# Letting GpSimd take turns between the passes of two score tiles, with eight constants of the planner set anew, in a window attention kernel whose score tiles are shared by three engines

## The chip, the cores and the metric

One core of a Trainium2 chip. The metric is the device time of one execution in microseconds (us), lower is better. The kernel before takes 1082.78 us (median of 3 runs, 1082.43 to 1082.89).

## The reference

Cross-shaped window attention on a 224 x 224 image with 96 channels. Half of the channels attend within horizontal stripes of 8 rows, half within vertical stripes of 8 columns; each stripe has 1792 tokens.

```python
qkv = einsum('bhwc,cd->bhwd', x, wqkv)             # x: (1, 224, 224, 96) bf16
# per direction: 28 stripes of 8*224 = 1792 tokens, 48 channels
a = softmax(einsum('bqc,bkc->bqk', q, k) * 48**-0.5)
o = einsum('bqk,bkc->bqc', a, v)
# ... the two halves are put side by side ...
return einsum('bhwc,cd->bhwd', o, wo)
```

What matters here: the scores' exponential. Two stripes are worked on together, and their scores are cut into tiles of 128 partitions x 1024 values; there are 28 pairs x 49 = 1372 such tiles.

## The kernel before

A planner inside the kernel runs when the program is built. It keeps a modelled time for each engine, picks the next instruction of each, and so writes one fixed order per engine with semaphore waits. A score tile goes to one of three engines:

- ScalarE ("a"): one exponential instruction out of PSUM.
- VectorE ("d"): an approximation in four passes over the tile, which stays in PSUM banks 4 and 5 meanwhile.
- GpSimd ("p"): VectorE copies the tile from banks 4 and 5 into a z buffer in SBUF, and GpSimd makes six passes there.

The last pass writes the bits of a bf16 number as an integer; a second matmul then multiplies the tile with V.

```python
NZP = 2                                            # z buffers
zp_sb = [sb(f"zp_sb{i}", [128, 1024], FP32) for i in range(NZP)]
up_sb = sb("up_sb", [128, 1024], FP16)             # one set of scratch
uq_sb = sb("uq_sb", [128, 1024], FP16)
# ...
def add(eng, waits, fn, occ=100.0, done=None, mode=None):
    # ... occ: how long the plan has the engine taken;
    # without done, the result is visible to others at occ + 100 ns
# ...
def p_dur(k):                                      # planned ns of a GpSimd pass
    return 1047.0 if k in (0, 2, 5) else 2130.0

def p_step(e, k, zi, sl):                          # pass 1 is k == 0
    z = zp_sb[zi][:]
    frac = zp_sb[zi][:].bitcast(U16)[:, 0:2048:2]
    u, q = up_sb[:], uq_sb[:]
    if k == 0: return e.tensor_scalar(u, frac, PS / U, PS * PA, ALU.mult, ALU.add)
    if k == 1: return e.tensor_tensor(q, u, u, ALU.mult)
    if k == 2: return e.tensor_scalar(q, q, 1.0, PB, ALU.mult, ALU.add)
    if k == 3: return e.tensor_tensor(u, q, u, ALU.mult)
    if k == 4: return e.tensor_tensor(z, z, u, ALU.add)
    return e.tensor_scalar(PTP[sl][:].bitcast(U16), z, 1.0, PC, ALU.mult, ALU.add)

def pick_pool():                                   # t is the plan's time
    # ... an output addition first, if one is ready ...
    if pow_q:
        p = pow_q[0]                               # the oldest tile, until it is done
        if vis(p["ev"]) > t:                       # its last pass isn't visible yet
            return False
        # ... plan pass p["k"], waiting for p["ev"] ...
```

GpSimd also makes the output additions ("L647") of the second, vertical half. Numbering of the passes: pass 1 to 6 are L983, L985, L987, L989, L991, L992 in the kernel before. In the changed one they are L985, L987, L989, L991, L993, L994, and the copy is L1037 in place of L1033.

The softmax here doesn't subtract the row's maximum and nothing guards it: scores larger than these inputs give would overflow.

## Time and profile before

| | before |
|---|---|
| time, median | 1082.78 us |
| span of the profiled run | 1081.0 us |
| score tiles: ScalarE / VectorE / GpSimd | 1161 / 117 / 94 |
| ScalarE's exponentials, busy and idle before them | 1064.7 us and 1.9 us |
| GpSimd busy | 959.3 us |

The tile counts are the counts (x...) of the exponential, of VectorE's first pass and of GpSimd's first pass. GpSimd's waits in the kernel before (who waited for whom: total us, times, longest us):

```profile
POOL up_sb L983 <- DVE zp_sb L1033: 47.7, 6, 38.6
POOL out_sb L647 <- DVE tmp L624: 22.3, 26, 4.4
```

38.6 us of the first line is the one wait for the very first tile. What is left, 9.1 us for copies and 22.3 us for output additions, is nearly all that the view puts down to other engines in the rest of the run (TensorE adds 1.3 us).

### The profile page before, as it was taken

The numbers are of one execution on the slowest core, as the hardware profiler recorded it, in microseconds if no ns is written. First come the engines' busy times: TensorE is split into PE (matmuls) and PEld (weight loads), VectorE is DVE, ScalarE is ACT, GpSimd is POOL, SyncE is SP. The second block draws the span as 40 slices with busy tenths as digits, with TensorE's granted clock in tenths as the row PEclk, the third lists the DMA queues.
The fourth block names the chain that finished last, engine by engine and source line by source line (L and its number), as shares of the span: only waits on it lengthen the run. The fifth ranks groups of instructions, "written<-read, shape, count | busy, mean of one in ns | idle before, by whom it ended". The sixth has DMA issues, their size and how long they took to land.

```text
span 1081.0 us, 28395 instructions
## 1 busy us (share of the span) xinstructions
PE 1030.4 (95%) x12065; PEld 374.3 (35%) x12065; DVE 1025.8 (95%) x1411; ACT 1066.9 (99%) x1164; POOL 959.3 (89%) x662
## 2 busy tenths in 40 slices
PE   9999999999999999999999999999999999999997
PEld 3333333333333333333333333333333333333332
DVE  6999999999999999999999999999999999999997
ACT  7999999999999999999999999999999999999997
POOL 0499999989998999998998999999999999999995
PEclk9999999999999999999999999999999999999999
DMA  5301101110110121011011222222222222221111
GB/s 98 76 6 36 36 10 27 36 28 10 36 36 11 26 36 19 18 36 21 19 34 32 39 42 41 40 41 41 40 42 40 39 43 40 39 42 37 34 22 33
DMA packets 168999, 37.35 MB, mean 35 GB/s; under 512 B 168872, under 2 KB 168872, under 8 KB 168872
## 3 DMA queue, kind: packets, MB, share of 16 engines
q1 hardware_dynamic: 167256, 35.35, 17.1%
q8 instruction: 94, 1.54, 0.6%
q10 hardware_dynamic: 1616, 0.18, 0.1%
q14 instruction: 33, 0.27, 0.1%
HBM read 0.15 MB, written 9.63 MB: 9 GB/s over the span
## 4 chain that ended last, share of the span: by engine, by line
ACT 97%; SPq 1%; PE 0%; DMA 0%; DVE 0%; issue 0%
ACT PTA L892 97%; SPq L205 1%; DMA xT_sb<-in_x_dram 0%; PE ps L853 0%; PE ps L198 0%; DVE tmp L624 0%; DVE out_sb L647 0%; PE ps L612 0%; PE ps L1176 0%; DVE OT_sb L943 0%; PE ps L467 0%; DVE rc L618 0%; PE ps L724 0%
## 5 line engine op out<-in xcount | busy, mean ns | idle before, releaser
L892 ACT ACTIVATE PTA<-ps 128x1024 bf16<-128x1024 f32 x1161 | 1064.7, 1290 | 1.9 <-PE ps L198 1.9
L198 PE MATMUL ps<-QT_sb,KT_sb 49*64 49x512 bf16 (+3 forms) x5488 | 476.3, 363 | 43.3 <-ACT PTA L892 32.2
L853 PE MATMUL ps<-PTA,V_sb 128*64 128x512 bf16 (+1 forms) x2648 | 412.1, 365 | 0.2
L194 PEld LDWEIGHTS <-KT_sb 49*64 49x64 bf16 (+1 forms) x5488 | 138.3, 103 | 324.9 <-issue 312.8
L989 POOL TENSOR_TENSOR up_sb<-uq_sb,up_sb 128x1024 f16<-128x1024 f16 x94 | 200.2, 2130 | 7.0
L991 POOL TENSOR_TENSOR zp_sb<-zp_sb,up_sb 128x1024 f32<-128x1024 f32 x94 | 200.5, 2133 | 6.3
L853 PEld LDWEIGHTS ps<-PTA,V_sb 128*64 128x64 bf16 x2648 | 119.0, 108 | 197.8 <-issue 155.7
L985 POOL TENSOR_TENSOR uq_sb<-up_sb 128x1024 f16<-128x1024 f16 x94 | 178.1, 1894 | 7.3
L911 DVE TENSOR_SCALAR tt_sb<-ps 128x1024 f32<-128x1024 uint16 x117 | 142.8, 1221 | 11.1 <-PE ps L198 6.6
L983 POOL TENSOR_SCALAR up_sb<-zp_sb 128x1024 f16<-128x1024 uint16 x94 | 98.4, 1047 | 54.2 <-DVE zp_sb L1033 47.7
L913 DVE SCALAR_TENSOR_TENSOR sq_sb<-ps,tt_sb 128x1024 f32<-128x1024 uint16 x117 | 142.1, 1214 | 0.2
L916 DVE TENSOR_TENSOR PTD<-tt_sb,ps 128x1024 uint16<-128x1024 f32 x117 | 141.6, 1211 | 0.4
L915 DVE TENSOR_TENSOR tt_sb<-sq_sb,ps 128x1024 f32<-128x1024 f32 x117 | 141.6, 1210 | 0.1
L1033 DVE COPY zp_sb<-ps 128x1024 f32<-128x1024 f32 x94 | 114.9, 1223 | 18.6 <-PE ps L198 14.2
L647 POOL TENSOR_TENSOR out_sb<-tmp,Ph_sb 128x480 bf16<-128x480 f32 (+2 forms) x89 | 86.6, 977 | 24.7 <-DVE tmp L624 22.3
L987 POOL TENSOR_SCALAR uq_sb<-uq_sb 128x1024 f16<-128x1024 f16 x94 | 98.4, 1047 | 8.2
L992 POOL TENSOR_SCALAR PTP<-zp_sb 128x1024 uint16<-128x1024 f32 x94 | 98.4, 1047 | 8.2
L467 PE MATMUL ps<-xT_sb,w_sb 128*64 128x448 bf16 (+3 forms) x448 | 84.0, 372 | 0.7 <-DMA xT_sb<-in_x_dram 0.5
L492 DVE SCALAR_TENSOR_TENSOR KT_sb<-ksum,ps 128x448 bf16<-128x448 f32 (+1 forms) x112 | 68.7, 613 | 3.6 <-PE ps L467 2.7
L943 DVE CAST OT_sb<-ps 128x512 bf16<-128x512 f32 (+5 forms) x118 | 69.3, 591 | 1.0 <-PE ps L853 0.7
L624 DVE TENSOR_TENSOR tmp<-ps,rc 128x480 f32<-128x480 f32 (+2 forms) x92 | 53.7, 583 | 3.1
L584 DVE TENSOR_TENSOR Ph_sb<-ps,rc 128x480 bf16<-128x480 f32 x84 | 52.4, 624 | 2.9
(52 smaller groups left out, 616.1 us busy)
## 6 DMA issues: line engine op xcount, KB each, us to landing
out_dram<-out_sb SPq DMA_DIRECT2D x389, 24.0 KB, 1.9
xT_sb<-in_x_dram SPq DMA_TRANSPOSE x332, 2.5
w_sb<-in_wqkv_dram ACTq DMA_DIRECT2D x2, 54.0 KB, 3.3
out_dram<-out_sb ACTq DMA_DIRECT2D x3, 24.0 KB, 1.9
wo_sb<-in_wo_dram SPq DMA_DIRECT2D x4, 9.0 KB
wo_sb<-one_sb SPq DMA_DIRECT2D x4, 0.0 KB
```

The source lines that it names most:

```text
L194: return e.add_instruction(mybir.InstLdweights(tile_size=(64, 64), tile_position=pos, name=nc.get_next_instruction_name(), engine=mybir.En ...
L198: return e.add_instruction(mybir.InstMatmult(start_tensor_calc=True, stop_tensor_calc=True, tile_size=(64, 64), tile_position=pos, ldweigh ...
L853: ins = e.matmul(bk[64 * wdw:64 * wdw + 64, 0:qs], lhsT=V_sb[b][:, wdw, kt, :], rhs=pt[:, wdw * 512 + i * qs:wdw * 512 + (i + 1) * qs], st ...
L892: e = add("act", [ev, bufA_ev[sl]], lambda e, base=base, sl=sl: e.activation(PTA[sl][:], ps[:, base * 512:(base + 2) * 512], ACTF.Exp, sca ...
L911: return lambda e: e.tensor_scalar(tt_sb[:], frac, (HA + RT) * U, CD / U ** 3, ALU.add, ALU.mult)
L913: return lambda e: e.scalar_tensor_tensor(sq_sb[:], frac, (HA - RT) * U, tt_sb[:], ALU.add, ALU.mult)
L915: return lambda e: e.tensor_tensor(tt_sb[:], sq_sb[:], frac, ALU.mult)
L916: return lambda e: e.tensor_tensor(PTD[sl][:].bitcast(U16), tt_sb[:], dps, ALU.add)
L985: return e.tensor_tensor(q, u, u, ALU.mult)
L989: return e.tensor_tensor(u, q, u, ALU.mult)
L991: return e.tensor_tensor(z, z, u, ALU.add)
L1033: ev = add("dve", [d["prev"], zp_rd[zi]], lambda e: e.tensor_copy(zp_sb[zi][:], dps), D_OCC[0], D_OCC[0] + 107.0)
```

## The change

Its intent: two tiles are in work at once, and GpSimd gives them passes in turn. Then no pass follows the pass that it depends on, and the gap between two dependent passes is filled. That needs a set of scratch for each tile. Eight constants of the planner were set anew with it.

```diff
-    SLACK = 160
+    SLACK = 120
-    GRP = 3
+    GRP = 2
-    NBP = 3
+    NBP = 2
-    DUES = 2.5
-    DUE1 = 5
+    DUES = 1
+    DUE1 = 0
-    LATE = 10
-    UTH = 2
+    LATE = 5
+    UTH = 4
-    WARM = 600
+    WARM = 400
 ...
-        up_sb = sb("up_sb", [128, 1024], FP16)
-        uq_sb = sb("uq_sb", [128, 1024], FP16)
+        up_sb = [sb(f"up_sb{i}", [128, 1024], FP16) for i in range(NZP)]
+        uq_sb = [sb(f"uq_sb{i}", [128, 1024], FP16) for i in range(NZP)]
 ...
-                        zi = D["np"] % NZP
+                        zi = min(set(range(NZP)) - set(zp_use))
+                        zp_use.append(zi)
 ...
-            if pow_q:
-                p = pow_q[0]
+            for p in sorted(pow_q, key=lambda p: p["turn"]):
                 zi, k = p["zi"], p["k"]
                 if vis(p["ev"]) > t:
-                    return False
+                    continue
 ...
                 p["k"] += 1
+                p["turn"] = cnt["pool"]
```

More of the change, by code (lines that the diff above doesn't have):

```diff
@@ L736, in bass_standalone__window_attn_cswin__vision_kernel @@
         zp_rd = [None] * NZP
+        zp_use = []
         P_n = [0]
@@ L980, in p_step @@
             frac = zp_sb[zi][:].bitcast(U16)[:, 0:2048:2]
-            u, q = up_sb[:], uq_sb[:]
+            u, q = up_sb[zi][:], uq_sb[zi][:]
             if k == 0:
@@ L1011, in pick_pool @@
                         if bufP_ev[sl] is None or vis(bufP_ev[sl]) > t:
-                            return False
+                            continue
                         ws.append(bufP_ev[sl])
@@ L1017, in pick_pool @@
                 p["k"] += 1
+                p["turn"] = cnt["pool"]
                 if p["k"] == PN:
                     P_n[0] += 1
-                    pow_q.pop(0)
+                    pow_q.remove(p)
                     pt_ev[p["G"]] = (ev, PTP[sl], ("p", sl))
                     zp_rd[zi] = ev
+                    zp_use.remove(zi)
                     P_out.remove(p["G"])
@@ L1035, in do_d @@
                 D["cur"] = None
-                pow_q.append(dict(G=d["G"], zi=zi, k=0, ev=ev))
+                pow_q.append(dict(G=d["G"], zi=zi, k=0, ev=ev, turn=0))
                 return True
```

## The prediction

> **What bounds the kernel now.** I read the chain that ended last first, then the groups of instructions, then GpSimd's own timeline.
>
> ```profile
> ACT 97%; SPq 1%; PE 0%; DMA 0%; DVE 0%; issue 0%
> L892 ACT ACTIVATE PTA<-ps 128x1024 bf16<-128x1024 f32 x1161 | 1064.7, 1290 | 1.9 <-PE ps L198 1.9
> ...
> L911 DVE TENSOR_SCALAR tt_sb<-ps 128x1024 f32<-128x1024 uint16 x117 | 142.8, 1221 | 11.1 <-PE ps L198 6.6
> L983 POOL TENSOR_SCALAR up_sb<-zp_sb 128x1024 f16<-128x1024 uint16 x94 | 98.4, 1047 | 54.2 <-DVE zp_sb L1033 47.7
> ...
> L1033 DVE COPY zp_sb<-ps 128x1024 f32<-128x1024 f32 x94 | 114.9, 1223 | 18.6 <-PE ps L198 14.2
> L647 POOL TENSOR_TENSOR out_sb<-tmp,Ph_sb 128x480 bf16<-128x480 f32 (+2 forms) x89 | 86.6, 977 | 24.7 <-DVE tmp L624 22.3
> ```
>
> ScalarE is the chain: 97% of it, with 1.9 us of idle before its exponentials. The problem has 1372 score tiles (28 window pairs of 49), and each is exponentiated by one of three engines: 1161 by ScalarE, 117 by VectorE (four passes), 94 by GpSimd (a VectorE copy, then six passes). 1161 + 117 + 94 = 1372. ScalarE's tiles overlap (1290 ns each, 1064.7 us for all), so one costs 1064.7 / 1161 = 0.917 us. So the time is about 1064.7 us plus start and tail (1081.0 - 1064.7 = 16.3 us of the span), and **the only lever of size is how many tiles leave ScalarE**. 2% of 1082.78 us is 21.7 us, or 24 tiles.
>
> GpSimd is busy for 959.3 us of 1081.0, so 121.7 us idle. 38.6 of them are the one wait for the first tile (longest wait in the waits view). The rest shows in its timeline (start, length, engine, line). First a tile in the first half, then a stretch in the second half, where output additions (L647) come between passes:
>
> ```profile
> 508.61 1.05 POOL L992 TENSOR_SCALAR PTP<-zp_sb 128x1024 uint16<-128x1024 f32 x1
> 509.74 1.05 POOL L983 TENSOR_SCALAR up_sb<-zp_sb 128x1024 f16<-128x1024 uint16 x1
> 510.87 1.89 POOL L985 TENSOR_TENSOR uq_sb<-up_sb 128x1024 f16<-128x1024 f16 x1
> 512.85 1.05 POOL L987 TENSOR_SCALAR uq_sb<-uq_sb 128x1024 f16<-128x1024 f16 x1
> 513.98 2.13 POOL L989 TENSOR_TENSOR up_sb<-uq_sb,up_sb 128x1024 f16<-128x1024 f16 x1
> 516.19 2.13 POOL L991 TENSOR_TENSOR zp_sb<-zp_sb,up_sb 128x1024 f32<-128x1024 f32 x1
> 518.41 1.05 POOL L992 TENSOR_SCALAR PTP<-zp_sb 128x1024 uint16<-128x1024 f32 x1
> 519.54 1.05 POOL L983 TENSOR_SCALAR up_sb<-zp_sb 128x1024 f16<-128x1024 uint16 x1
> ```
>
> ```profile
> 650.86 2.13 POOL L991 TENSOR_TENSOR zp_sb<-zp_sb,up_sb 128x1024 f32<-128x1024 f32 x1
> 652.95 1.10 POOL L647 TENSOR_TENSOR out_sb<-tmp,Ph_sb 128x480 bf16<-128x480 f32 x1
> 654.13 1.05 POOL L992 TENSOR_SCALAR PTP<-zp_sb 128x1024 uint16<-128x1024 f32 x1
> ...
> 666.28 1.05 POOL L983 TENSOR_SCALAR up_sb<-zp_sb 128x1024 f16<-128x1024 uint16 x1
> 667.29 1.10 POOL L647 TENSOR_TENSOR out_sb<-tmp,Ph_sb 128x480 bf16<-128x480 f32 x1
> ```
>
> A tile takes 519.54 - 509.74 = 9.80 us, of which its passes fill 9.30; the other 0.5 is six gaps of 0.08. Where an independent L647 follows L983 or L991, it starts 0.04 us *before* the recorded end (667.29 against 666.28 + 1.05): about 0.12 us is won there. But L992 followed by the next tile's L983 is independent too (the copy was done microseconds earlier) and still has the gap: 509.74 - 508.61 - 1.05 = 0.08. Over all adjacent pairs in the timeline the rule holds: **next to L987 and L992 the gap of 0.08 stays on either side, dependent or not**; between the other passes it turns into an overlap of 0.04 when the neighbour is independent.
>
> **What the Trainium skill says.** (1) "GPSIMD Engine Reference", section 2.1 Instruction dispatch: completion gates what waits on the instruction's semaphore and does not hold back the next Pool instruction. The trace agrees beside L983, L985, L989 and L991 (-0.04 us) and differs beside L987 and L992 (+0.08 us), for which I have no reason. (2) "Perfetto Trace Analysis", section GPSIMD Engine Instruction: time these by start-to-start spacing, not by recorded length; I do. (3) "SBUF — State Buffer", section Who interferes with whom: a VectorE instruction with two SBUF inputs contends with GpSimd's reads, one with at most one outside the two-port modes does not. VectorE's passes here each read PSUM and at most one SBUF tile, and GpSimd's L991 stays within 2124 to 2141 ns over all 94: the trace agrees, so more GpSimd work should not slow VectorE.
>
> **The change part by part.** *No arithmetic changes*: the six passes, their sizes and their count per tile are the same. Added is one more pair of fp16 scratch tiles and the alternation.
>
> *Directly on the chip.* Two tiles fully alternating have 12 boundaries. Four of the 12 passes are L987 or L992; if none are neighbours they touch 8 boundaries, if they pair up, 6. So 4 to 6 boundaries gain 0.12 us: 0.48 to 0.72 us for two tiles, 0.24 to 0.36 us per tile, that is 9.80 to about 9.5 us. This is far less than if every gap vanished.
>
> *Through the static plan.* The instruction order is fixed at build time by a planner in the kernel that gives a pass 1047 or 2130 ns and makes its result visible 100 ns later. Alone, a tile is planned at 3 x 1047 + 3 x 2130 + 6 x 100 = 10,131 ns, although the chip needs 9.80 us. That overestimate of 0.33 us over 94 tiles is 31 us, and the trace shows GpSimd waiting for about that much: 24.7 us before L647 and 54.2 - 38.6 = 15.6 us before L983 (6.5 of it the plain gaps). Alternating, the 100 ns hide under the other tile's pass and the plan needs only 9,531 ns. Real cost when alternating (9.5) or alone (9.80) is about at or below what is planned, so the plan isn't too optimistic and the chip should not fall behind it.
>
> *How often are two tiles on hand?* Only two z buffers exist (the count is unchanged). One is freed at the end of L992 and refilled by a matmul and a VectorE copy, which share the two PSUM banks with VectorE's own tiles. From the starts and ends of all copies and last passes: the copy ends on average 6.6 us after the finish that freed its buffer, and 4.5 us before its tile's first pass. So in a period of 9.8 us, two tiles are on hand for about 4.5 us, or 46%; for the rest one tile runs alone with its gaps. The plan then saves not 0.60 but about 0.28 us per tile in the present rhythm, up to 0.6 at best.
>
> *The sum.* GpSimd's planned budget is 94 x 10.13 = 952 us. At 9.85 us a tile it holds 96.7, at 9.53 it holds 99.9: **3 to 6 more tiles on GpSimd, I take 4.5**, of which part comes from retuning. Each costs VectorE a copy; successive VectorE passes start 1.13 us apart, so a copy is a quarter of a VectorE tile (4 x 1.13), and VectorE is 96% busy in the middle (115 of 120 us). So ScalarE loses 0.75 to 1 tile for each: 3.4 to 4.5 tiles, times 0.917 = 3.1 to 4.1 us. I take 3.6 us.
>
> *The retuned constants* (SLACK, GRP, NBP 3 to 2, DUES, DUE1, LATE, UTH, WARM) change when fills and second matmuls are placed. ScalarE waits only 1.9 us, so they can't win there; they can win VectorE tiles: it waits 14.2 us and 6.6 us for score matmuls before L1033 and L911. I give them nothing up or down, but they widen the range. 1082.8 - 3.6 = 1079.2; I say **1079.2 us**.
>
> **The rivals.** (a) *Refill becomes the wait*: alternating, both tiles hold their buffers to near the end, VectorE's copy comes late, and GpSimd runs one tile alone most of the time. For: the 6.6 us above. Against: it cannot be worse than now, since a lone tile goes as before. Then 0 to 1 us is won: 1082. (b) *VectorE becomes the limit*: each new tile's copy displaces VectorE passes; already in the sum as 0.75. With three more misfit waits at two result buffers instead of three, the gain may be 1 to 2 us: 1081. (c) *GpSimd really fills up*: both tiles are on hand throughout, 6 tiles or more, and retuning adds VectorE tiles; VectorE's 4% of idle would hold at most 5 to 7 tiles more. That is the best case, 10 tiles or 9 us: 1073. (d) *Plan and chip part*: late result tiles stall TensorE and then ScalarE. Against: GpSimd's tiles are taken 24 tiles ahead, and the planned times are not below the measured ones.
>
> **Range and chances.** Rival (a) or a small regression in tuning sets the upper end, 1082.9; half of (c) the lower, 1075. Even (c) in full stays under 2%, because GpSimd's 121.7 us of idle hold at most 12 tiles, 11 us. Slower by 2% would need ScalarE to stall for over 21 us, of which there is no sign. Faster by over 2%: 1%; within 2%: 98.5%; slower: 0.5%.
>
> **What would show it.** Right: the count of L983 rises to 97 to 100, VectorE's L911 falls by 0 to 2, L892 falls by 3 to 5 and still takes 0.917 us each; in the timeline passes of two tiles alternate for about half of the time; gaps of 0.08 remain beside L987 and L992, overlaps of 0.04 stand elsewhere; GpSimd's waits before L647 shrink. Wrong: gaps that vanish beside L987 and L992 too; L983 waiting for copies by much more than 9 us after the first; ScalarE idle above 5 us; or L892's count unchanged or down by more than 7, which would mean that the retuned constants, not the alternation, set the time.

## The result, and the profile after

The changed kernel takes 1081.41 us (median of 4 runs, 1081.01 to 1081.62), the kernel before beside it 1082.61 us (4 runs). A ratio in this document is the mean time of one kernel's fast runs over that of the other's of the same rounds, so it is not quite the ratio of the medians. Here it is 0.9988, with a 95% interval of 0.9971 to 1.0006. A second study of the same kernel (after_again, below) gives 1081.49 us and 0.9989, 0.9977 to 1.0001. So the change is worth about 1.2 us, a ninth of a per cent; the intervals just reach 1, although no run of the changed kernel was as slow as any run of the kernel before.

From the page of the changed kernel, the lines that answer to those of before: the chain that ended last, and the groups (count, then busy us and mean ns, then idle us before them with the main releaser):

```profile
ACT 98%; PE 1%; DVE 0%; DMA 0%; issue 0%; POOL 0%
...
L894 ACT ACTIVATE PTA<-ps 128x1024 bf16<-128x1024 f32 x1160 | 1063.7, 1291 | 1.9 <-PE ps L198 1.9
...
L913 DVE TENSOR_SCALAR tt_sb<-ps 128x1024 f32<-128x1024 uint16 x115 | 140.4, 1221 | 13.4 <-PE ps L198 9.5
L985 POOL TENSOR_SCALAR up_sb<-zp_sb 128x1024 f16<-128x1024 uint16 x97 | 101.4, 1045 | 49.6 <-DVE zp_sb L1037 48.2
```

GpSimd has three tiles more (97), VectorE two fewer (115), so ScalarE has **one** fewer (1160). Its busy time falls by 1064.7 - 1063.7 = 1.0 us, and this is nearly the whole difference in time. ScalarE is as much the bound as before.

GpSimd's timeline in the changed kernel (start and length in us, engine, line), where two tiles alternate:

```profile
524.15 1.04 POOL L985 TENSOR_SCALAR up_sb<-zp_sb 128x1024 f16<-128x1024 uint16 x1 [0.65 <-DVE zp_sb L1037]
525.16 2.13 POOL L993 TENSOR_TENSOR zp_sb<-zp_sb,up_sb 128x1024 f32<-128x1024 f32 x1
527.24 1.90 POOL L987 TENSOR_TENSOR uq_sb<-up_sb 128x1024 f16<-128x1024 f16 x1
529.22 1.04 POOL L994 TENSOR_SCALAR PTP<-zp_sb 128x1024 uint16<-128x1024 f32 x1
530.35 1.04 POOL L989 TENSOR_SCALAR uq_sb<-uq_sb 128x1024 f16<-128x1024 f16 x1
531.48 2.13 POOL L991 TENSOR_TENSOR up_sb<-uq_sb,up_sb 128x1024 f16<-128x1024 f16 x1
```

Pass 5 of one tile (L993) starts at 525.16, 0.03 before the recorded end of pass 1 of the other (524.15 + 1.04). But beside passes 3 and 6 (L989, L994) the gap stays although the neighbours belong to different tiles: 530.35 - 529.22 - 1.04 = 0.09. Over the whole trace, from the first tile on, 256 boundaries overlap now and 361 have a gap of about 0.08, against 83 and 532 before. The 173 overlaps more are worth about 173 x 0.12 = some 20 us of GpSimd's time. And at the top, what comes with it: a first pass that waits 0.65 us for VectorE's copy. The waits view of the changed kernel:

```profile
POOL up_sb L985 <- DVE zp_sb L1037: 48.2, 23, 30.5
POOL out_sb L647 <- DVE tmp L624: 14.0, 20, 3.2
```

The first tile comes 8.1 us earlier (30.5 against 38.6). Of the other copies, GpSimd waits for 22 and 17.7 us, against 5 and 9.1 us before. Counting from the ends of copies and last passes, two tiles lie in the z buffers for 651 of 1029 us (63%), against 411 of 1025 us (40%) before.

### The profile page after: what moved, and what is told of

The parts are those of the page before. It is cut to its first block, busy times and chain, and to the rows that moved or that the text cites. A ratio compares the mean times of both kernels' runs of the same rounds, so it can differ in the third digit from the quotient of the medians.

```text
span 1079.2 us, 28435 instructions
## 1 busy us (share of the span) xinstructions
PE 1029.2 (95%) x12067; PEld 373.4 (35%) x12067; DVE 1021.4 (95%) x1406; ACT 1065.9 (99%) x1163; POOL 979.4 (91%) x680
## 4 chain that ended last, share of the span: by engine, by line
ACT 98%; PE 1%; DVE 0%; DMA 0%; issue 0%; POOL 0%
ACT PTA L894 98%; PE ps L240 0%; PE ps L198 0%; PE ps L1071 0%; DMA out_dram<-out_sb 0%; PE ps L467 0%; DVE out_sb L647 0%; DVE tmp L624 0%; PE ps L428 0%; PE ps L855 0%; DVE KT_sb L515 0%; DVE KT_sb L492 0%; PE ps L612 0%; POOL out_sb L647 0%; DVE rc L618 0%
## 5 line engine op out<-in xcount | busy, mean ns | idle before, releaser
L894 ACT ACTIVATE PTA<-ps 128x1024 bf16<-128x1024 f32 x1160 | 1063.7, 1291 | 1.9 <-PE ps L198 1.9
L198 PE MATMUL ps<-QT_sb,KT_sb 49*64 49x512 bf16 (+3 forms) x5488 | 474.9, 364 | 42.8 <-ACT PTA L894 32.1
L991 POOL TENSOR_TENSOR up_sb<-uq_sb,up_sb 128x1024 f16<-128x1024 f16 x97 | 206.4, 2128 | 5.1
L993 POOL TENSOR_TENSOR zp_sb<-zp_sb,up_sb 128x1024 f32<-128x1024 f32 x97 | 206.8, 2132 | 3.0
L987 POOL TENSOR_TENSOR uq_sb<-up_sb 128x1024 f16<-128x1024 f16 x97 | 183.6, 1893 | 3.5
L913 DVE TENSOR_SCALAR tt_sb<-ps 128x1024 f32<-128x1024 uint16 x115 | 140.4, 1221 | 13.4 <-PE ps L198 9.5
L985 POOL TENSOR_SCALAR up_sb<-zp_sb 128x1024 f16<-128x1024 uint16 x97 | 101.4, 1045 | 49.6 <-DVE zp_sb L1037 48.2
L915 DVE SCALAR_TENSOR_TENSOR sq_sb<-ps,tt_sb 128x1024 f32<-128x1024 uint16 x115 | 139.8, 1216 | 0.4
L917 DVE TENSOR_TENSOR tt_sb<-sq_sb,ps 128x1024 f32<-128x1024 f32 x115 | 139.3, 1211 | 0.2
L1037 DVE COPY zp_sb<-ps 128x1024 f32<-128x1024 f32 x97 | 118.6, 1223 | 18.2 <-PE ps L198 13.6
L994 POOL TENSOR_SCALAR PTP<-zp_sb 128x1024 uint16<-128x1024 f32 x97 | 101.3, 1044 | 8.1
L989 POOL TENSOR_SCALAR uq_sb<-uq_sb 128x1024 f16<-128x1024 f16 x97 | 101.3, 1044 | 7.9
L647 POOL TENSOR_TENSOR out_sb<-tmp,Ph_sb 128x480 bf16<-128x480 f32 (+2 forms) x89 | 86.5, 976 | 16.1 <-DVE tmp L624 14.0
```

What stands on the lines that cost most here:

```text
L198: return e.add_instruction(mybir.InstMatmult(start_tensor_calc=True, stop_tensor_calc=True, tile_size=(64, 64), tile_position=pos, ldweigh ...
L894: e = add("act", [ev, bufA_ev[sl]], lambda e, base=base, sl=sl: e.activation(PTA[sl][:], ps[:, base * 512:(base + 2) * 512], ACTF.Exp, sca ...
L913: return lambda e: e.tensor_scalar(tt_sb[:], frac, (HA + RT) * U, CD / U ** 3, ALU.add, ALU.mult)
L915: return lambda e: e.scalar_tensor_tensor(sq_sb[:], frac, (HA - RT) * U, tt_sb[:], ALU.add, ALU.mult)
L917: return lambda e: e.tensor_tensor(tt_sb[:], sq_sb[:], frac, ALU.mult)
L1037: ev = add("dve", [d["prev"], zp_rd[zi]], lambda e: e.tensor_copy(zp_sb[zi][:], dps), D_OCC[0], D_OCC[0] + 107.0)
```

## The experiments

The question: the alternation does on the chip what it was meant to. Why does so little come of it, and is that little due to the alternation? Theory 1: ScalarE's tile count sets the time, and that count comes from the planner's constants as much as from the alternation. Its rival is my prediction's: the alternation frees GpSimd time, and that time turns into tiles. Theory 2, put beside it for the runs on the chip's side: GpSimd has slack against the fixed order, so that gaps matter only through the plan. Theory 3 was formed after the run chained: the plan fills GpSimd so far that there is little slack. All runs gave correct results. "As built" in an expectation means the count in the built program, which the run's page then confirmed.

### after_again, alt_only, consts_only: the parts of the change

after_again is the changed kernel unchanged.

> The changed kernel once more, for a tighter interval (first ratio 0.9988, interval 0.9971 to 1.0006). ScalarE has 1160 tiles against 1161. Theory 1 (the count of ScalarE's tiles sets the time): -0.9 us plus what start and tail give, a ratio of 0.9985 to 0.9992. Rival (the difference is noise between runs): the interval holds 1.0.

Measured: 1081.49 us against 1082.68 (before, 11 runs), ratio 0.9989, 0.9977 to 1.0001.

alt_only takes the changed code with the old constants (put on one line here):

```diff
-    SLACK = 120; GRP = 2; NBP = 2; DUES = 1;   DUE1 = 0; LATE = 5;  UTH = 4; WARM = 400
+    SLACK = 160; GRP = 3; NBP = 3; DUES = 2.5; DUE1 = 5; LATE = 10; UTH = 2; WARM = 600
```

> The changed code with all eight constants as before. As built, ScalarE gets 1162 tiles, VectorE 117, GpSimd 93. Theory 1 (count of ScalarE's tiles sets the time, and the alternation by itself frees nothing that the plan can use): 0.9 us slower than before, 1083.5 us, ratio 1.0005 to 1.0015. Rival (my prediction's: the alternation takes gaps out of GpSimd's work and so out of the time): 1 to 3 us faster than before. Gaps in GpSimd should shrink in either case; under theory 1 its waits for VectorE's copy or additions grow by about as much.

consts_only takes the old code with the new constants, that is the same edit to the kernel before, in the other direction.

> The kernel before with the eight new constants, one tile at a time on GpSimd. As built, ScalarE gets 1163 tiles, VectorE 115, GpSimd 94. Theory 1: 1.8 us slower than before, 1084.4 us, ratio 1.001 to 1.0025. Rival (the constants are what is worth something): 1 us or more faster than before.

Measured: alt_only 1084.05 us, ratio 1.0013 (1.0001 to 1.0025); consts_only 1086.05 us, ratio 1.0031 (1.0019 to 1.0043). **Each part alone is a little slower than the kernel before.** From the page of alt_only, groups as above:

```profile
L894 ACT ACTIVATE PTA<-ps 128x1024 bf16<-128x1024 f32 x1162 | 1065.5, 1298 | 1.9 <-PE ps L198 1.9
...
L985 POOL TENSOR_SCALAR up_sb<-zp_sb 128x1024 f16<-128x1024 uint16 x93 | 97.2, 1045 | 72.6 <-DVE zp_sb L1037 66.5
L913 DVE TENSOR_SCALAR tt_sb<-ps 128x1024 f32<-128x1024 uint16 x117 | 142.9, 1221 | 17.8 <-PE ps L198 12.7
...
L647 POOL TENSOR_TENSOR out_sb<-tmp,Ph_sb 128x480 bf16<-128x480 f32 (+2 forms) x88 | 86.1, 981 | 30.8 <-DVE tmp L624 28.9
```

With the old constants the alternation leaves GpSimd 93 tiles, one fewer than before, and ScalarE 1162. The overlaps are there (214 against 83), but the time they save is spent in waits: 66.5 - 38.8 (the first tile) = 27.7 us for copies against 9.1 before, and 30.8 us before L647 against 24.7. Two tiles in step with each other free their z buffers late and close together (30 last passes end within 5 us of the one before, none did in the kernel before), and no tile at all is in the buffers for 47 us, against 9 us before. My rival (a), that the refill becomes the wait, is what happens here. consts_only has 1163 tiles on ScalarE (1.8 us by the count), and the tail after its last exponential is 7.7 us against 6.2, which is nearly all of its other 1.6 us. From its page:

```profile
L892 ACT ACTIVATE PTA<-ps 128x1024 bf16<-128x1024 f32 x1163 | 1066.5, 1295 | 2.1 <-PE ps L198 2.1
...
L911 DVE TENSOR_SCALAR tt_sb<-ps 128x1024 f32<-128x1024 uint16 x115 | 140.5, 1222 | 18.4 <-PE ps L198 13.7
L983 POOL TENSOR_SCALAR up_sb<-zp_sb 128x1024 f16<-128x1024 uint16 x94 | 98.2, 1044 | 52.2 <-DVE zp_sb L1033 34.5
```

So the new constants alone take VectorE from 117 tiles to 115, with GpSimd's 94 unchanged; alt_only keeps VectorE's 117. From consts_only to the changed kernel the alternation is the only difference. There it brings GpSimd three tiles, takes three off ScalarE and none off VectorE: 1086.05 to 1081.49, **4.6 us faster**. With the old constants the same alternation costs 1.4 us. Neither part has a worth of its own; the 1.2 us belong to the two together.

### chained and chain_passes: is the missing gap worth anything on the chip?

Both keep the changed kernel's order on every engine and put dependences back in. chained makes every GpSimd instruction wait for the one before it:

```diff
+            if eng == "pool" and cnt[eng]:
+                waits.append((SEMS[eng], cnt[eng], 0.0))
             cnt[eng] += 1
             ops[eng].append((waits, fn, True))
```

> The changed kernel with exactly its order of instructions on every engine, but every GpSimd instruction also waits for the one just before it, so that all gaps come back (some 0.12 us at each boundary that now overlaps, roughly 20 us over the run). Theory 2 (the gain comes through the plan's counts alone; GpSimd has slack against the fixed plan): the same time as the changed kernel within 0.5 us, and GpSimd's waits before L647 and the first pass shrink by what the gaps take. Rival (the chip needs the gaps gone to keep up with the plan): 2 to 10 us slower than the changed kernel, with ScalarE or TensorE waiting for late GpSimd tiles.

Measured: 1116.98 us (1109.79 to 1125.36), ratio 1.0311 (1.0272 to 1.035): far beyond what either theory expected. It turned out to be too strong a dose. A first pass or an addition that now waits for VectorE and for GpSimd has a gap of 0.15 us, not of 0.08 (the trace shows its wait for GpSimd in a semaphore instruction of its own). From the median gap of each kind of boundary I work out some 42 us more GpSimd time in all, in place of the 20 intended. The chain of the run and the waits show how it reaches ScalarE (this kernel's lines are 2 higher):

```profile
ACT 52%; POOL 23%; PE 16%; DVE 6%; issue 2%; DMA 0%; POOLq 0%; DVEq 0%
```

```profile
DVE zp_sb L1039 <- POOL PTP L996: 20.4, 22, 2.4
PE ps L200 <- ACT PTA L896: 22.4, 67, 0.5
ACT PTA L896 <- PE ps L200: 17.0, 30, 1.6
```

VectorE stands still in its fixed order before a copy, because GpSimd's last pass has not yet freed the z buffer (20.4 us in 22 waits; before, 0.7 us once). Everything that VectorE evacuates comes later, then score matmuls, then ScalarE, which waits 17.0 us here and 8.7 us on a second line of matmuls; its busy time is 8.4 us longer too. The granted clock fell too, to 0.98 in the mean; how much of the 35 us is due to that I did not separate.

chain_passes is the right dose: only passes 2 to 6 wait for the instruction before them, which replaces a wait that they have anyway.

```diff
+                if k:
+                    ws.append((SEMS["pool"], cnt["pool"], 0.0))
                 ev = add("pool", ws, lambda e: p_step(e, k, zi, sl), p_dur(k))
```

> As chained, but milder: only the second to sixth pass of a tile also waits for the GpSimd instruction just before it, first passes and output additions do not, so that no instruction has one wait more than it had and each gap is the 0.08 us that the kernel before has. In the changed kernel's timeline 144 boundaries into second, fourth and fifth passes overlap by 0.04; they become gaps of 0.08: 144 x 0.12 = 17 us more for GpSimd in all. The changed kernel's GpSimd waits 17.7 us for copies (after the first tile) and 16.1 us before L647. Theory 3 (GpSimd is filled by the plan so far that the fixed order has little slack): 3 to 20 us slower than the changed kernel, with ScalarE waiting for score matmuls by several us. Theory 2 (the slack hides it; the 35 us of chained came from its doubled waits): within 1 us of the changed kernel.

Measured: 1081.83 us (4 runs), ratio to before 0.9991 (0.9977 to 1.0006): **the same as the changed kernel, 1081.49 us**. In its timeline the gaps are back at passes 2, 4 and 5 (0.08 where it was -0.04, 17 us in all), and in its waits the slack has taken them:

```profile
POOL up_sb L985 <- DVE zp_sb L1039: 37.5, 8, 31.7
POOL out_sb L647 <- DVE tmp L624: 9.9, 11, 3.2
```

37.5 - 31.7 = 5.8 us for copies in place of 17.7, and 9.9 us before additions in place of 14.0. So as long as GpSimd keeps ahead of the fixed order, the overlaps buy no time directly. VectorE's copy waits 6.8 us in all for z buffers now (12 times; 0.6 us once in the changed kernel), while ScalarE's idle time before its exponentials is 0.1 us longer. Theory 3 was too strict: 17 us fit in, 42 us do not.

### strided and single_op: what keeps the gap beside passes 3 and 6?

strided lays uq_sb out with a step of two elements; single_op turns pass 3 into one operation.

```diff
-        uq_sb = [sb(f"uq_sb{i}", [128, 1024], FP16) for i in range(NZP)]
+        uq_sb = [sb(f"uq_sb{i}", [128, 2048], FP16) for i in range(NZP)]
-            u, q = up_sb[zi][:], uq_sb[zi][:]
+            u, q = up_sb[zi][:], uq_sb[zi][:, 0:2048:2]
```

> The changed kernel with the scratch uq_sb laid out with a step of two elements, so that L989 reads and writes 2-byte values 4 bytes apart, as L985 reads its input. Same order and counts. If the contiguous form is what keeps the gap: gaps beside L989 go from +0.08 to -0.04 where the neighbour is independent. If it is not: they stay. Time the same within 1 us as long as the passes take as long as before.

```diff
-                return e.tensor_scalar(q, q, 1.0, PB, ALU.mult, ALU.add)
+                return e.tensor_single_scalar(q, q, PB, ALU.add)
```

> The changed kernel with L989 as one addition in place of a multiplication by 1 and an addition. If the two-operation form keeps the gap: gaps beside L989 go to -0.04. If it is not: they stay at +0.08. L985 has two operations and no gap, so I expect no change. Time the same within 1 us.

Neither removes the gap: beside pass 3 it stays at 0.08 in either (for single_op that was expected), so its cause is open. The time, expected within 1 us, is a miss in both, because pass 3 got longer. The group of it, first in strided, then in single_op:

```profile
L989 POOL TENSOR_SCALAR uq_sb<-uq_sb 128x1024 f16<-128x1024 f16 x97 | 130.2, 1342 | 7.9
```

```profile
L989 POOL TENSOR_SCALAR uq_sb<-uq_sb 128x1024 f16<-128x1024 f16 x97 | 268.5, 2768 | 7.9
```

Against 1044 ns these are 97 x 0.298 = 29 us and 97 x 1.724 = 167 us more. The times (one run each, state unknown) are 1088.7 and 1248.31 us. They give the dose curve a second half: 17 us more GpSimd time cost about 0.3 us, 29 us cost 7, 42 us cost 35, 167 us cost 167. **By these runs GpSimd's slack in the changed kernel lies between 17 and 29 us, somewhat less than its waits after the first tile (17.7 + 16.1 us); beyond it, late GpSimd work stops ScalarE.** It is no exact curve: the doses delay different instructions, and the upper end rests on one run.

### b_meas: take the slack away in a serial plan

The kernel before, with pass times in the plan that make a lone tile 9.80 us, as measured:

```diff
         def p_dur(k):
-            return 1047.0 if k in (0, 2, 5) else 2130.0
+            return (1030.0, 1880.0, 1030.0, 2110.0, 2120.0, 1030.0)[k]
```

> The kernel before, one tile at a time and its own constants, with only the plan's pass times set so that a lone tile is planned at 9.80 us as the trace has it, in place of 10.13. As built: ScalarE 1160, VectorE 116, GpSimd 96. My prediction held that the 31 us of overestimate are wasted. Theory 2: then 0.9 us faster than before, 1081.8 us, without any alternation, the same as the change brings. Theory 3 (the overestimate is the slack that keeps GpSimd ahead of the fixed order): 1 us or more slower than before, with ScalarE idle above 5 us.

Measured: 1086.62 us, ratio 1.0037 (1.0024 to 1.005): 4 us slower than before, though ScalarE has one tile fewer. The group of the exponentials and the wait of VectorE's copy for GpSimd:

```profile
L892 ACT ACTIVATE PTA<-ps 128x1024 bf16<-128x1024 f32 x1160 | 1065.3, 1250 | 4.7 <-PE ps L198 4.0
```

```profile
DVE zp_sb L1033 <- POOL PTP L992: 7.7, 11, 1.0
```

The same wait as in chained appears, 7.7 us where the kernel before has 0.7. ScalarE's idle time reaches 4.7 us (1.9 before), a little under the 5 that I had expected for theory 3, its busy time is 0.6 us longer in spite of the tile fewer, and the tail is 0.4 us longer. Together these are 3.8 of the 4 us. So the overestimate in the plan is not simply wasted: it is slack, and the dose curve and this run agree in that. But the sum of VectorE's waits is no measure of what is lost (chain_passes has 6.8 us of them and loses 0.3 us), and one more thing stays open: a new plan differs in more than its slack, as the longer tail of consts_only shows.

### serial_tuned: the same gain without the alternation?

The kernel before, serial and with its planned pass times, with twelve constants drawn at random; of 500 draws that were built (not run), the one whose plan ends first:

```diff
+    SLACK = 120; DSLACK = 150; GRP = 3; NBP = 2; DUES = 1; DUE1 = 2; LATE = 0
+    UTH = 4; LOOKP = 22; HOLD = 125; FDUE = 15; WARM = 400
```

> The kernel before, one tile at a time on GpSimd with one set of scratch, with twelve constants drawn anew (the best of 500 draws by the plan's own end). As built: ScalarE 1160, VectorE 117, GpSimd 95; ScalarE's count is that of the changed kernel. Theory A (what the change gained is the draw of constants, and a serial order can have it too): 1081.5 us, within 0.5 us of the changed kernel. Theory B (only the alternation gives GpSimd the room for it): 1082.5 us or more, with ScalarE waiting for late tiles as in b_meas.

Measured: 1081.74 us (1081.6 to 1082.15), ratio 0.9994 (0.998 to 1.0008). That is 0.25 us from the changed kernel, and the two intervals lie mostly over each other (the kernel before of its own rounds took 1082.52 us, so it gains 0.8 us beside it):

```profile
L892 ACT ACTIVATE PTA<-ps 128x1024 bf16<-128x1024 f32 x1160 | 1063.8, 1273 | 2.6 <-PE ps L198 2.6
```

**One tile at a time gets ScalarE down to the same 1160 tiles**, with 117 on VectorE and 95 on GpSimd. So the count does not need the alternation. Whether the alternation helps on average over many draws of the constants is shown by no run.

### one_z: what a GpSimd tile is worth

```diff
-    NZP = 2
+    NZP = 1
```

> The kernel before with a single z buffer, which takes GpSimd down to 62 tiles: a lever for what a GpSimd tile is worth. As built: ScalarE 1181, VectorE 129. My prediction's exchange (a copy costs a quarter of a VectorE tile): 32 tiles fewer should give VectorE 8 and ScalarE 24, 1104.7 us. The two PSUM banks that both share (2.10 us held for a GpSimd tile, 7.32 us for a VectorE tile in the trace of before): 32 x 2.10 / 7.32 = 9.2 more for VectorE and 22.8 for ScalarE, 1103.6 us. As built the exchange is 12 and 20, 20 x 0.917 = 18.3 us: 1101.0 us if the count alone sets the time.

Measured: 1101.4 us (4 runs), ratio 1.0175 (1.0161 to 1.0189). From its page:

```profile
L892 ACT ACTIVATE PTA<-ps 128x1024 bf16<-128x1024 f32 x1181 | 1082.9, 1294 | 1.9 <-PE ps L198 1.9
...
L911 DVE TENSOR_SCALAR tt_sb<-ps 128x1024 f32<-128x1024 uint16 x129 | 157.7, 1222 | 21.5 <-PE ps L198 15.1
```

32 tiles fewer on GpSimd put 12 on VectorE and 20 on ScalarE: 18.9 us, against 20 x 0.917 = 18.3 by the count. A GpSimd tile takes 0.63 of a tile off ScalarE here and costs VectorE 0.38 of a tile, not a quarter. Neither exchange in the expectation fits: they gave VectorE 8 and 9.2 tiles more, it got 12. Part of the difference may lie in PSUM banks 4 and 5, which one tile holds at a time. From the end of one tile's last VectorE instruction to the end of the next one's, a GpSimd tile holds them 2.10 us and a VectorE tile 7.32 us in the kernel before. 94 x 2.10 + 116 x 7.32 (the first tile can't be measured so) = 1046 us, and the ratio of holds is 0.29. That the sum fills the run is no finding, because each hold begins where the one before ends. But counted only from a tile's first score matmul on (the records of L198 with 50 rows), the banks still hold a tile for 981 of the 1046 us. VectorE itself is busy for 1025.8 us, so whether the banks or VectorE's time set the exchange stays open.

### alt_mid and alt_meas: can it be turned into time?

Both have the alternating order and constants drawn anew. The plan gets separate times for "GpSimd is free again" and "the result is visible": as measured in alt_meas, a little longer in alt_mid.

```diff
-                ev = add("pool", ws, lambda e: p_step(e, k, zi, sl), p_dur(k))
+                ev = add("pool", ws, lambda e: p_step(e, k, zi, sl), P_OCC[k], P_DONE[k])
# alt_mid
+        P_OCC = (1045.0, 1900.0, 1200.0, 2110.0, 2110.0, 1200.0)
+        P_DONE = (1145.0, 1995.0, 1145.0, 2230.0, 2230.0, 1145.0)
+    SLACK = 120; DSLACK = 135; GRP = 3; NBP = 2; DUES = 1; DUE1 = 2; LATE = 10
+    UTH = 2; LOOKP = 22; HOLD = 140; FDUE = 15; WARM = 600
# alt_meas
+        P_OCC = (1015.0, 1855.0, 1130.0, 2090.0, 2090.0, 1130.0)
+        P_DONE = (1130.0, 1980.0, 1130.0, 2215.0, 2215.0, 1130.0)
+    SLACK = 100; DSLACK = 135; GRP = 3; NBP = 3; DUES = 1; DUE1 = 5; LATE = 5
+    UTH = 4; LOOKP = 21; HOLD = 160; FDUE = 15; WARM = 600
```

> The alternating order with the plan's pass times between the measured and the old ones (9.51 us for a tile that alternates, 9.85 us for one alone), and constants drawn anew (best of 1500). As built: ScalarE 1158, VectorE 116, GpSimd 98. If the slack suffices: 3 x 0.917 = 2.8 us faster than before, 1079.9 us. If it does not: ScalarE waits above 4 us and the time is 1082 us or more.

> The alternating order with the plan's pass times as measured (starts 1.015, 1.855, 1.13, 2.09, 2.09, 1.13 us apart when alternating, 9.80 us for a tile alone) and constants drawn anew (best of 500). As built: ScalarE 1157, VectorE 116, GpSimd 99. Count alone: 3.7 us faster than before, 1079.0 us. As b_meas showed, a plan without slack loses 2 to 8 us in waits: then 1081 to 1087 us.

Measured: alt_mid **1080.23 us** (1079.56 to 1080.55), ratio 0.9979 (0.9965 to 0.9992), the fastest kernel; alt_meas 1085.7 us (1085.39 to 1090.12), ratio 1.0034 (1.002 to 1.0048). The groups of alt_mid, then the exponentials in alt_meas (its page is that of the slowest of its five runs, 1090.12 us):

```profile
L894 ACT ACTIVATE PTA<-ps 128x1024 bf16<-128x1024 f32 x1158 | 1062.0, 1267 | 2.2 <-PE ps L198 2.2
...
L913 DVE TENSOR_SCALAR tt_sb<-ps 128x1024 f32<-128x1024 uint16 x116 | 141.7, 1221 | 14.3 <-PE ps L198 9.7
...
L985 POOL TENSOR_SCALAR up_sb<-zp_sb 128x1024 f16<-128x1024 uint16 x98 | 102.4, 1045 | 37.8 <-DVE zp_sb L1037 36.6
```

```profile
L894 ACT ACTIVATE PTA<-ps 128x1024 bf16<-128x1024 f32 x1157 | 1063.1, 1257 | 10.4 <-PE ps L198 7.8
```

In alt_meas one tile more is off ScalarE, and no slack is left: 10.4 us of idle eat it and more. alt_mid gains 2.3 us for three tiles. Its four tiles more on GpSimd cost VectorE one, so 0.75 of a tile leaves ScalarE for each; the five of alt_meas take four off ScalarE, 0.8 for each. Whether a serial plan with similar constants would reach 1158 tiles with enough slack was not run, so I can't say how much of alt_mid's gain needs the alternation.

## Why the prediction was right or wrong

The time, 1081.41 us, lies in the range (1075.0 to 1082.9), and "within 2%" with the chance of 98.5% was right. The predicted gain of 3.6 us was three times the measured 1.2 us. Part of the hit is luck: the range reached up to 1082.9, so no change at all would have lain in it too. Of the signs that it named, the 97 tiles, the two that VectorE lost, the gaps and the shorter waits before additions came true; ScalarE's fall of 3 to 5 tiles did not, and one sign of being wrong appeared, waits for copies "by much more than 9 us after the first": 17.7 us. By its steps:

- **ScalarE's count is the only lever: right.** ScalarE idles 1.9 us before its exponentials in both kernels, and 1160 tiles in place of 1161 are 0.92 of the 1.2 us. one_z confirms it over 20 tiles: 18.9 us measured, 18.3 by the count. With other plans it is not the only one: consts_only loses 1.5 us to its tail, b_meas 2.8 us to idle time.
- **The gap rule (0.08 stays beside passes 3 and 6, elsewhere -0.04): right**, in every run. The 20 us won on the chip are 20 / 97 = 0.21 us per tile, just below the predicted 0.24 to 0.36, because two tiles were on hand 63% of the time and not always. I had taken 46% for that; it was more.
- **"3 to 6 more tiles on GpSimd, I take 4.5": mis-sized.** It got 3, partly by luck: 8.1 us of their time is the earlier first tile, nothing that the prediction had. It comes with the constants: the longest wait is 31.0 us in consts_only, 38.8 in alt_only.
- **"So ScalarE loses 0.75 to 1 tile for each": for the change as a whole, this step failed.** Three more tiles took one off ScalarE, because VectorE lost two. I had counted only the time of the copies on VectorE (1.13 of 4.52 us each). But it is not the copies that took those two tiles: consts_only has VectorE's 115 without any tile more on GpSimd, and from there to the changed kernel three tiles take three off ScalarE. alt_mid and alt_meas give 0.75 and 0.8; one_z, a large step the other way, gives 0.63, and b_meas one tile for two. So the predicted exchange is one of several that the runs show, and it was not the copies but the constants that made it small here.
- **"That overestimate of 0.33 us over 94 tiles is 31 us" (of waits, which the change would use): right in size, wrong in use.** Taken away in b_meas, with one tile fewer on ScalarE, the time rose by 4 us. The changed kernel did not use it up either: its waits after the first tile are 17.7 + 16.1 = 33.8 us; before they were 9.1 + 24.7 = 33.8 us.
- **"I give them nothing up or down" (the constants): wrong, and this is the term that the sum lacked.** Alone they cost two VectorE tiles and 3.4 us. The prediction thought that they could win VectorE tiles, which waited 6.6 us for score matmuls before L911; in consts_only that wait is 13.7 us. But it is 12.7 us in alt_only, which keeps its 117 tiles, so why VectorE loses two, and by which of the eight constants, stays open. The alternation on top of them is worth 4.6 us, more than the 3.6 predicted (three tiles are 2.8 of it, a tail 1.6 us shorter the rest), and the two together 1.2 us. In the other order the alternation costs 1.4 us and the constants win 2.6, so the two can't be credited apart; and twelve other constants give a serial order the same 1160 tiles.
- **Rival (a), "refill becomes the wait": I gave it too little.** It is what alt_only shows in full, and the changed kernel in part (17.7 us for copies against 9.1).
- **Rival (d), "plan and chip part": rightly held unlikely for this change**, and b_meas, chained and alt_meas show what it looks like. But I expected late results to stop TensorE. What stops first is VectorE, at its copy into a z buffer that is not yet free.

Where the expected gain went: GpSimd did win some 20 us on the chip. With the old constants waits for copies and additions took it; with the new ones it became, together with the earlier first tile, three tiles. These make good the two tiles that the same constants take from VectorE, and one is left over for ScalarE.

## What to carry to other kernels

Filling a gap on an engine that is off the critical path buys nothing by itself; ask which count or wait on the bounding engine it will change, and run the idea and the accompanying retuning each without the other before crediting either. In a statically ordered program an overestimated duration is slack: measure how much delay the engine can bear before making the plan exact. When work moves between engines, take its price from runs between which nothing else changes: three GpSimd tiles took one off ScalarE beside the kernel before, and three beside the kernel with the same constants.

## What the Trainium skill lacked or had wrong

- "GPSIMD Engine Reference", section 2.1: it says that completion does not hold back the next Pool instruction. Beside passes 1, 2, 4 and 5 and the additions that holds (the next one starts 0.03 to 0.05 us before the recorded end). It lacks that passes 3 and 6, both a TENSOR_SCALAR, keep 0.08 us on either side with an independent neighbour too (pass 1, a TENSOR_SCALAR as well, does not); a stepped layout or a single operation did not remove it beside pass 3.
- "GPSIMD Engine Reference", section 4.1, calls one-input operations roughly line-rate. One addition on 128x1024 fp16 took 2768 ns, while a multiplication by 1 and the addition in one instruction took 1044 ns.
- "GPSIMD Engine Reference", section 7, puts the cost of a stepped access at a byte step over 8. That is about reads, and pass 1, which reads 2-byte values 4 bytes apart and writes contiguously, agrees with it (1045 ns). It lacks stepped writes: pass 3 with that step on both sides took 1342 ns in place of 1044, which points to the write and was not tried with the write alone.
- No page that I read has this: a GpSimd instruction that waits for the one just before it starts 0.08 us after that one's end when it carries this wait itself, even with a second wait in a semaphore instruction of its own ahead of it (43 second passes of chained). Where the wait for the one before stands in that separate instruction, as in the first passes and additions of chained, it starts 0.14 to 0.16 us after, and 0.17 with a third wait (11 additions).
